# A new hand-searched order for a fused attention and gated-MLP kernel, with the normalization of v taken off GpSimd and two scalar loads issued late

## The chip, the cores and the metric

One Trainium2 chip; the program runs on one of its cores. The metric is device time in microseconds (us), the median of several runs. A profiled execution gives the trace from which the rows below are taken.

## The reference, cut to what matters

```python
# attention: B=4, H=8, S=768, D=64; the first 4 keys (sinks) and a window of 128 keys are kept
scores = scale * q @ k.T
keep = (pos < n_sink) | ((rel >= 0) & (rel < window))
a = exp(where(keep, scores, -1e9) - max); a = a / (sum(a) + 1e-9)
x = (a @ v).transpose(0, 2, 1, 3).reshape(B, S, 512)
# gated MLP: d_ff = 1024
h = maximum(x @ w_in, 0); u, v = h[..., :512], h[..., 512:]
v_n = (v - mean(v)) / sqrt(var(v) + 1e-6)          # over the last axis
v_s = einsum('ts,bsd->btd', w_spatial, v_n) + b_spatial[None, :, None]
out = (u * v_s) @ w_out
```

n_sink and window arrive as 64-bit integers, w_in and w_out as 64-bit floats.

## The kernel before, in words

The four batches b are cut into six blocks t of 128 rows. For each block and each half of the heads (hf) there is one piece of work of each kind: a score product on TensorE into four PSUM banks (tile `sc`), four masks on VectorE that also give the row maximum (`pexp`, `nm`), four exponentials on ScalarE, a split of the result into two 16-bit parts (`p`), a transpose, and the product with v (`av`). Then follow the block's `x`, its half of the first MLP product that gives v (`ps_v`), the relu into `vr`, the statistics on VectorE, the "root" (the power -1/2 of the variance, one GpSimd instruction, `rs`), the "norm" (subtract the mean, multiply by the root) and the split into `vn`. `ps_u`, `ps_s`, `ps_o` are the other products of the MLP; `ps_s` of a batch needs all six `vn` of it. Three PSUM banks serve the MLP products, so TensorE can be three such products ahead of the engines that read them.

At the start the weights are decoded: each 128x512 piece of w_in is loaded as 512 KB of 64-bit words (`dec`), and three engines make 32-bit floats of it: `wtmp` on ScalarE (L546), `w` on VectorE (L548, L551), the sum on GpSimd (L554). The first two blocks work on 32-bit data, the later ones on 16-bit pairs. The first key and query block is loaded in four pieces of 128 KB, two each on the queues of SyncE (SP) and ScalarE; all other loads and all transposes go through SP's queue.

No scheduler decides the order. `plan.add` gathers some 1,800 numbered pieces of work, each with the engines that may do it, and the table `ORDER` lists them in the order in which they are recorded: a number, a letter for the engine (d VectorE, a ScalarE, p GpSimd, P TensorE, S the SP queue), and for some TensorE pieces a count of filler matmuls (`P22`: 22 small products with the identity, line L438, ahead of the piece). Each engine takes its own pieces strictly in this order. The durations given to `plan.add` play no part when the kernel is built.

`load_scalars` brings the two scalar words n_sink and window to all partitions (`words`). They are read by one late VectorE piece (`wf`, L650) that goes into the flag which tells whether the fast path's result holds.

Of the kernel before, what the change touches and what calls it, by code (L numbers as in the profile page):

```python
# [6 lines left out]
F32 = mybir.dt.float32  # L7
# [3 lines left out]
I32 = mybir.dt.int32  # L11
# [8 lines left out]
P = 128  # L20
# [218 lines left out]
185P22:188 171P 214a 8a 221a 37d 225d 30d 157d 36a 108a 223a 234a 29a 31d 224p 256S 226S 222S 32p 10d 11p 187d
232a 230a 236a 237a 57S 50a 239a 238S 210a 261P 268d 262d 266d 188P3 189a 264d 241d 240p 242S 51d 109d 38d 39p  # L240
211d 144P 145d 12a 33a 269a 265a 263a 267a 270p 277P2:192 280d 284d 282d 363S 278d 34d 192P 272a 273p 52d 53p
227P 274d 318P 323d 271S 190a 191d 244d 283a 243P 281a 259a 275S 285a 40a 279a 286a 54p 193a 324a 325d 326a 290p
288a 289p 321d 322a 319d 320a 329a 497S 330p 245d 260d 55d 327a 331p 41d 313S 316a 146P 334P 341d 342a 337d 335d
246P 5a 339d 340a 194d 276P 201P 202a 336a 147a 247a 13d 317d 287S 367P 374d 6d 372d 368d 370d 293d 195p 196p
291S 338a 19a 343a 20d 345a 346p 205P 206a 203P 347p 248d 148d 292P 294d 383P 388d 362S 390d 384d 249P 498a 369a
371a 505S 386d 56S 328S 332S 333P 506p 550S 344S 63a 64d 375a 507p 373a 376a 378a 379d 348S 295P 204a 377S 380d
149p 150p 381S 387a 151p 197p 552S 510P 515d 511d 152p 517d 296d 513d 199P 297d 385a 349P 389a 391a 392a 394a
553p 395p 350d 351d 250a 251d 393S 200a 396p 397S 524P 525d 514a 365a 58S 305P 366d 298P 529d 531d 527d 554p 306a
# [69 lines left out]
1764d 1765a 1766d 1754P 1755a 1313S 1756S 1287S 1767P 1768d 1769p 1770a 1772P 1773d 1774p 1656P 1654P 1655a 1771d  # L318
1775d 1776d 1783P 1784d 1785p 1793P 1794d 1786a 1787d 1652P 1653d 1788P 1789d 1790p 1791d 1780P 1781a 1782S 1792d
1795p 1777P 1796a 1797d 1657a 1798P 1799d 1778a 1800p 1808P 1803P 1801a 1802d 1810P 1813a 1779S 1814S 1804P 1805a  # L320
1806S 1807P 1809P 1811d 1812S
"""


# [919 lines left out]
```

## Time and profile before

| what | value |
|---|---|
| median of 3 runs | 399.76 us (399.09 to 400.67) |
| the profiled execution's own time | 400.12 us |
| its span, first to last instruction | 398.3 us |
| TensorE busy | 387.3 us, 97% of the span |
| mean granted TensorE clock | 0.994 |

The span is shorter than the execution's own time by 1.8 us, which lie outside the instructions. A busy TensorE also counts a matmul that has been started and whose end is modelled, and it counts the filler matmuls.

### The profile page before, as it was taken

How to read it: one execution, taken by the hardware profiler on the slowest of the kernel's cores; microseconds unless marked ns; L12 is line 12 of the kernel's file. 1: busy time of each engine (PE TensorE's matmuls, PEld its weight loads, DVE VectorE, ACT ScalarE, POOL GpSimd, SP SyncE). 2: the span in 40 equal slices, each digit the busy share in tenths (PEclk: the TensorE clock that was granted, in tenths of full speed). 3: DMA queues.
4: the chain of work that ended last, by engine and by line, in shares of the span. 5: the costliest groups of instructions: out<-in, count | busy, mean ns of one | idle time of the engine just before them, and what ended most of it. 6: DMA issues, size and time to landing. Idle time of an engine off the chain costs nothing.

```text
span 398.3 us, 10079 instructions
## 1 busy us (share of the span) xinstructions
PE 387.3 (97%) x3682; PEld 276.9 (70%) x3682; DVE 323.4 (81%) x927; ACT 257.2 (65%) x726; POOL 220.2 (55%) x242
## 2 busy tenths in 40 slices
PE   7999999899999999999999999999999999999995
PEld 4686676567786866577786767567785776586863
DVE  1899999799999999989899978889888899642231
ACT  2899897589679985887988658577852143111111
POOL 4347999597653775736693847483553543400210
PEclk9899999999999999999999999999999999999999
DMA  5999899999997979899999698698978985001102
GB/s 167 358 289 212 170 240 180 231 248 228 232 286 137 230 160 235 159 233 184 173 224 155 115 167 148 132 229 173 150 198 225 249 220 127 12 18 53 54 28 84
DMA packets 137767, 70.84 MB, mean 178 GB/s; under 512 B 112112, under 2 KB 125424, under 8 KB 137712
## 3 DMA queue, kind: packets, MB, share of 16 engines
q1 hardware_dynamic: 136880, 69.88, 79.4%
q8 instruction: 30, 0.49, 0.5%
q10 hardware_dynamic: 832, 0.26, 0.3%
q14 instruction: 25, 0.20, 0.2%
HBM read 36.57 MB, written 6.29 MB: 108 GB/s over the span
## 4 chain that ended last, share of the span: by engine, by line
PE 75%; DMA 9%; DVE 7%; ACT 5%; POOL 2%; issue 1%; SPq 1%; ACTq 0%; POOLq 0%; DVEq 0%
PE ps_s L527 23%; PE ps_o L1101 15%; PE ps_v L527 11%; PE ps_u L527 11%; PE sc L772 7%; DMA pT<-p 3%; ACT pexp L783 2%; DMA dec<-w_in 2%; PE av L898 2%; PE av L899 2%; PE av L900 2%; DVE pexp L777 2%; DMA kring<-qk_t 2%; DMA wsp<-w_sp_t 2%; DMA pexp<-w_in 1%
## 5 line engine op out<-in xcount | busy, mean ns | idle before, releaser
L783 ACT ACTIVATE pexp<-pexp,nm 128x260 f32<-128x260 f32 (+1 forms) x192 | 92.6, 484 | 18.6 <-DVE nm L777 18.4
L527 PE MATMUL ps_s<-wsp,vn 128*128 128x256 f16 x864 | 100.0, 273 | 0.0
L527 PEld LDWEIGHTS <-vn 128*128 128x128 f16 x864 | 83.5, 98 | 13.5 <-issue 1.5
L527 PE MATMUL ps_u<-xT,win 128*128 128x256 f16 x576 | 69.4, 273 | 0.3 <-ACT u L1051 0.2
L509 POOL TENSOR_TENSOR p<-pexp,p 128x16 f16<-128x16 f32 (+2 forms) x40 | 49.4, 1244 | 31.3 <-ACT p L493 24.4
L527 PEld LDWEIGHTS <-win 128*128 128x128 f16 x576 | 54.6, 98 | 12.1 <-issue 3.8
L1101 PE MATMUL ps_o<-wout,g 128*128 128x512 f16 x276 | 62.7, 379 | 0.0
L527 PE MATMUL ps_v<-win,xT 128*128 128x512 f16 x264 | 60.5, 379 | 0.0
L772 PE MATMUL sc<-kring 64*128 64x260 f16 (+3 forms) x480 | 46.9, 319 | 2.4 <-DVE nm L777 1.7
L1078 POOL TENSOR_TENSOR g<-g,u 128x256 f32<-128x256 f32 x27 | 22.1, 819 | 47.8 <-DVE g L1074 47.0
L1101 PEld LDWEIGHTS <-g 128*128 128x128 f16 x276 | 26.5, 98 | 29.6 <-issue 1.0
L527 PEld LDWEIGHTS <-xT 128*128 128x128 f16 x264 | 25.1, 98 | 28.4 <-issue 0.4
L1074 DVE SCALAR_TENSOR_TENSOR g<-ps_s,b_bc 128x256 f32<-128x256 f32 x48 | 20.0, 418 | 28.7 <-PE ps_s L527 28.6
L493 ACT CAST p<-pexp 128x32 f16<-128x32 f32 (+2 forms) x63 | 36.2, 595 | 5.3 <-DMA pT<-p 4.4
L783 ACT ACTIVATION_READ_ACCUMULATOR pexp<-pexp,nm 128x1 f32 x192 | 36.3, 189 | 0.0
L1017 POOL TENSOR_SCALAR vr<-vr,mv,rs 128x512 f32<-128x512 f32 x15 | 33.9, 2257 | 1.2
L675 ACT ACTIVATE g<-g 128x256 f16<-128x256 f32 x21 | 8.7, 413 | 39.8 <-POOL g L1078 22.6
L898 PE MATMUL av<-vring,pT 128*128 128x64 f16 x328 | 32.9, 193 | 0.0
L900 PE MATMUL av<-vring,pT 128*128 128x64 f16 x328 | 32.7, 193 | 0.0
L899 PE MATMUL av<-vring,pT 128*128 128x64 f16 x328 | 32.7, 193 | 0.0
L509 DVE TENSOR_TENSOR p<-pexp,p 128x1024 f16<-128x1024 f32 (+2 forms) x36 | 31.9, 898 | 0.5 <-ACT p L493 0.3
L898 PEld LDWEIGHTS <-pT 128*128 128x128 f16 x328 | 29.4, 98 | 1.9 <-issue 1.1
(146 smaller groups left out, 735.4 us busy)
## 6 DMA issues: line engine op xcount, KB each, us to landing
vraw<-v_s SPq DMA_DIRECT2D x30, 256.0 KB, 3.9
raw<-qk_t SPq DMA_DIRECT2D x12, 512.0 KB, 4.4
out<-ob SPq DMA_DIRECT2D x23, 256.0 KB, 2.4
kring<-qk_t SPq DMA_DIRECT2D x11, 512.0 KB, 6.9
dec<-w_in SPq DMA_DIRECT2D x8, 512.0 KB, 8.0
pexp<-w_in SPq DMA_DIRECT2D x8, 512.0 KB, 4.4
wsp<-w_sp_t SPq DMA_DIRECT2D x6, 384.0 KB, 4.1
dec<-w_out SPq DMA_DIRECT2D x4, 512.0 KB, 4.3
```

Source lines behind the costliest of these rows:

```text
L493: nc.scalar.copy(o, x)
L509: eng[e].tensor_tensor(out=o, in0=x, in1=hi, op=ALU.subtract)
L527: nc.tensor.matmul(o, a, m, start=(i == 0), stop=(i == n - 1))
L772: nc.tensor.matmul(view(h + q)[0], qq[:, hp, 1, 2:], keys, start=(j == 0), stop=(j == len(pairs) - 1))
L783: nc.scalar.activation(po, po, AF.Exp, bias=nm()[:, q:q + 1], scale=-1.0, accum_out=small_tile("sums", (b, t), H)[:, k:k + 1])
L898: nc.tensor.matmul(o[:, h], ph, vh, start=(t < 2 and j == 0), stop=False)
L899: nc.tensor.matmul(o[:, h], ph, vl, start=False, stop=False)
L900: nc.tensor.matmul(o[:, h], pl, vh, start=False, stop=(j == nb - 1 and (t < 2 or h == HH - 1)))
L1017: eng[e].tensor_scalar(vr(), vr(), vals["mv", i][:, 0:1], vals["rs", i], op0=ALU.subtract, op1=ALU.mult)
L1074: nc.vector.scalar_tensor_tensor(out=g(), in0=tl("ps_s", i)[:, :TC], scalar=G_S, in1=b_bc[:, t0:t0 + TC], op0=ALU.mult, op1=ALU.add)
L1078: eng[e].tensor_tensor(out=g(), in0=g(), in1=tl("u", (b, c0))[:, d, :], op=ALU.mult)
L1101: nc.tensor.matmul(o, lead, wout[:, w, d, :], start=(d == 0 and j == 0), stop=(d == KC - 1 and j == 2))
```

## The change

Four things change. The two word loads go from ScalarE's queue at the very start to SP's queue late in the program. The norm of v may run on ScalarE (as `scale * x + bias`) or VectorE instead of VectorE or GpSimd; for this, the root piece makes one more GpSimd value, `nb` = minus mean times root. The costs that the search for the order was given change at a few places. And the whole `ORDER` table is another one; its first two lines stand here for all 88.

```diff
 def load_scalars(nc, words, n_sink, window):
-    nc.scalar.dma_start(words[:, 0:2], n_sink.bitcast(I32).partition_broadcast(P))
-    nc.scalar.dma_start(words[:, 2:4], window.bitcast(I32).partition_broadcast(P))
+    nc.sync.dma_start(words[:, 0:2], n_sink.bitcast(I32).partition_broadcast(P))
+    nc.sync.dma_start(words[:, 2:4], window.bitcast(I32).partition_broadcast(P))
...
-114S 118P16 119d 123d 125d 124a 21S 23d 126a 121d 122a 120a 115S 116p 258p 209p 130P10:129 137d 22a 154S 110S
+114S 110S 118P12 115S 116p 117p 155p 111a 112d 121d 123d 119d 120a 125d 130P6:129 133d 135d 124a 122a 126a 127P
...
-            plan.add("check", last, 0, "d", 0.4, words, [], [("good", 0, 2)])
+            plan.add("w check", last, 0, "SP", 0.9, st.load_words, [], [("words", 0)], dma=2.0)
+            plan.add("check", last, 0, "d", 0.4, words, [("words", 0)], [("good", 0, 2)])
...
             def root(e):
-                nc.gpsimd.tensor_tensor(out=vals["rs", i], in0=vals["rs", i], in1=mhalf, op=ALU.pow)
+                rs = vals["rs", i]
+                nc.gpsimd.tensor_tensor(out=rs, in0=rs, in1=mhalf, op=ALU.pow)
+                vals["nb", i] = small.tile([P, 1], F32, tag="nb", name="nb")
+                nc.gpsimd.tensor_scalar(vals["nb", i], vals["mv", i][:, 0:1], rs, -1.0, op0=ALU.mult, op1=ALU.mult)
 
             def norm(e):
-                eng[e].tensor_scalar(vr(), vr(), vals["mv", i][:, 0:1], vals["rs", i], op0=ALU.subtract, op1=ALU.mult)
+                if e == "a":
+                    nc.scalar.activation(vr(), vr(), AF.Identity, bias=vals["nb", i], scale=vals["rs", i])
+                else:
+                    nc.vector.tensor_scalar(vr(), vr(), vals["mv", i][:, 0:1], vals["rs", i], op0=ALU.subtract, op1=ALU.mult)
...
-            plan.add("v root", r, b, "p", 0.535, root, [], [("st", i)])
-            plan.add("v norm", r, b, "dp", {"d": 0.47, "p": 2.05}, norm, [("st", i)], [("vr", i)], shared=True)
+            plan.add("v root", r, b, "p", 1.05, root, [], [("st", i)])
+            plan.add("v norm", r, b, "ad", {"a": 0.72, "d": 0.47}, norm, [("st", i)], [("vr", i)], shared=True)
...
-            load_scalars(nc, words, n_sink, window)
...
+            st.load_words = lambda e: load_scalars(nc, words, n_sink, window)
```

Counted over the two tables: of the 24 norms 15 stood on GpSimd and 9 on VectorE, and now 20 stand on ScalarE and 4 on VectorE; the filler matmuls go from 69 to 54 (16 to 12 ahead of the first scores, 10 to 6 ahead of the second, 12 to 8 and 22 to 14 around the first `av` products). Some 200 other pieces change their engine, in both directions; on balance VectorE gets 5 more low parts of `p` (28 of 44 instead of 23) and 6 more relus of u, and gives up 6 small sink parts.

VectorE at the start of the program, before: the masks of the first block (`m_first`, each with its `nm` row), and between them the first step of decoding weights.

```order
L777 ISA pexp,nm<-sc,m_first 128x128
L777 ISA nm 128x1
L548 TENSOR_SCALAR w_175<-dec 128x512
L777 ISA pexp,nm<-sc,m_first 128x128
L777 ISA nm 128x1
```

VectorE at the same place, now: the last mask of the first block, then the decoding, then the first mask of the second block (`m_second`).

```order
L778 ISA pexp,nm<-sc,m_first 128x128
L778 ISA nm 128x1
L548 TENSOR_SCALAR w_208<-dec 128x512
L551 SCALAR_TENSOR_TENSOR w_208<-dec,w_208 128x512
L778 ISA pexp,nm<-sc,m_second 128x260
```

Before, the decoding step stood ahead of five of the first block's eight masks; now it stands behind all eight. Ahead of the first mask there is now one step that waits for the small load `vsraw` (not in these rows).

ScalarE at the start, before: its two loads of the first keys, the two word loads, the table load, then the exponentials of the first block (L783) and the first decoding steps (L546).

```order
L1192 DMA kring<-qk_t 128x2x128 x2
L35 DMA words<-n_sink 128x2
L36 DMA words<-window 128x2
L1196 ACT_TABLE_LOAD
L1196 ACTIVATE first<-first 128x1
L783 ACTIVATE pexp,sums<-pexp,nm 128x128 x4
L546 ACTIVATE wtmp<-dec 128x512
L783 ACTIVATE pexp,sums<-pexp,nm 128x128 x4
L694 ACTIVATE vsink_134<-vsraw 96x256
```

ScalarE at the start, now, up to the first exponentials of the second block:

```order
L1199 DMA kring<-qk_t 128x2x128 x2
L1202 ACT_TABLE_LOAD
L1202 ACTIVATE first<-first 128x1
L695 ACTIVATE vsink_132<-vsraw 96x256
L784 ACTIVATE pexp,sums<-pexp,nm 128x128 x4
L546 ACTIVATE wtmp<-dec 128x512
L818 COPY pT<-pt 128x512
L784 ACTIVATE pexp,sums<-pexp,nm 128x128 x4
L546 ACTIVATE wtmp<-dec 128x512
L784 ACTIVATE pexp,sums<-pexp,nm 128x260 x2
```

The two word loads are gone from here, the step on `vsraw` came to the front, and the copy of the first transposed block (`pT`) came over from VectorE.

VectorE near the end, now, where the words are read (`wf`): the gates of the last batch (L1081) around it each free a bank of `ps_s`.

```order
L1081 SCALAR_TENSOR_TENSOR g<-ps_s,b_bc 128x256
L1093 SCALAR_TENSOR_TENSOR g_5931<-g_5931,g 128x256
L638 TENSOR_SCALAR good<-checks 128x31
L639 TENSOR_SCALAR good<-checks 128x12
L640 TENSOR_SCALAR good<-checks 128x12
L641 TENSOR_SCALAR good<-checks 128x12
L650 CAST wf<-words 128x4
L652 TENSOR_SCALAR good<-wf 128x1 x4
L1081 SCALAR_TENSOR_TENSOR g<-ps_s,b_bc 128x256
```

The reading of the words waited for nothing recent before; now it stands ahead of a gate and waits for a load that the SP queue issues some pieces earlier: in the table, TensorE has a `ps_u` and a `ps_s` between that issue and this row.

## Rows read from the trace of the kernel before

**Rows 1.** The page's first part: busy us, share of the span, instructions.

```profile
PE 387.3 (97%) x3682; PEld 276.9 (70%) x3682; DVE 323.4 (81%) x927; ACT 257.2 (65%) x726; POOL 220.2 (55%) x242
```

**Rows 2.** Waits of TensorE: us in total, times, longest.

```profile
PE pt L946 <- ACT vr L1001: 1.7, 1, 1.7
PE sc L772 <- DVE nm L777: 1.7, 1, 1.7
PE sc L772 <- DMA kring<-qk_t: 0.8, 1, 0.8
```

**Rows 3.** Windows: busy us of each engine, granted clock, DMA share, GB/s.

```profile
5.00:10.00 5.00, 3.81 (x25) 2.69 (x24) 1.03 (x7) 0.88 (x4) 0.80 (x6) 1.00 0.65 202
10.00:15.00 5.00, 4.10 (x19) 2.82 (x20) 3.22 (x16) 3.96 (x15) 1.88 (x2) 0.66 1.07 360
20.00:40.00 20.00, 19.95 (x183) 14.95 (x180) 19.81 (x58) 19.51 (x56) 12.01 (x13) 1.00 0.96 250
60.00:80.00 20.00, 17.56 (x183) 12.48 (x183) 16.70 (x57) 13.73 (x42) 15.28 (x16) 1.00 1.18 203
100.00:200.00 100.00, 100.00 (x1023) 70.36 (x1022) 93.70 (x251) 83.58 (x236) 63.11 (x64) 1.00 0.98 204
340.00:398.00 58.00, 53.97 (x405) 39.42 (x403) 19.59 (x49) 9.28 (x20) 10.35 (x15) 0.99 0.12 43
```

**Rows 4.** DMA issues of the first 4 us: queue, size, us to landing.

```profile
kring<-qk_t SPq DMA_DIRECT2D x1, 512.0 KB, 9.6
words<-n_sink ACTq DMA_DIRECT2D x1, 1.0 KB, 8.1
```

**Rows 5.** Timeline of the first 17 us, SP, ScalarE and VectorE: start, duration, what.

```profile
1.80 0.49 ACTq L35 DMA_DIRECT2D words<-n_sink  x1
2.25 0.67 SPq L736 DMA_DIRECT2D kring<-qk_t  x1
...
6.08 0.29 DVE L777 CUSTOM_DVE_ANT_0 pexp<-sc,m_first 128x128 f32<-128x128 f32 x1 [5.12 <-PE sc L772]
...
9.78 0.43 DVE L548 TENSOR_SCALAR w<-dec 128x512 int32<-128x512 int32 x1 [2.88 <-DMA dec<-w_in]
...
16.00 0.51 ACT L783 ACTIVATE pexp<-pexp,nm 128x260 f32<-128x260 f32 x1
```

**Rows 6.** Timeline of TensorE, first 31 us.

```profile
6.29 1.89 PE L438 MATMUL av<-ident 128*128 128x248 f16 x10
...
10.47 0.48 PE L772 MATMUL sc<-kring 64*128 64x128 f32 x2 [1.66 <-DVE nm L777]
...
13.05 1.84 PE L772 MATMUL sc<-kring 64*128 64x260 f32 x8
...
23.90 2.50 PE L438 MATMUL pt<-ident 128*128 128x248 f16 x22
```

**Rows 7.** Groups by line and form: count, busy us, mean ns.

```profile
L783 ACT ACTIVATE pexp<-pexp,nm 128x128 f32<-128x128 f32 x32 | 12.5, 392 | 7.9 <-DVE nm L777 7.8
L546 ACT ACTIVATE wtmp<-dec 128x512 int32<-128x512 uint32 x12 | 8.0, 667 | 0.9 <-DMA dec<-w_in 0.4 <-POOL w L554 0.4
L495 ACT ACTIVATE win<-w 128x512 f16<-128x512 f32 x6 | 3.6, 618 | 0.0
L817 ACT COPY pT<-pt 128x512 f32<-128x512 f32 x4 | 2.1, 577 | 0.7 <-PE pt L813 0.7
L1017 POOL TENSOR_SCALAR vr<-vr,mv,rs 128x512 f32<-128x512 f32 x15 | 33.9, 2257 | 1.2
L1014 POOL TENSOR_TENSOR rs<-rs,mhalf 128x1 f32<-128x1 f32 x24 | 18.4, 767 | 18.5 <-DVE rs L1011 17.5 <-DVE sums L905 1.0
L509 POOL TENSOR_TENSOR p<-pexp,p 128x1024 f16<-128x1024 f32 x17 | 36.8, 2163 | 22.1 <-ACT p L493 15.5 <-issue 5.9 <-DVE p L498 0.6
```

**Rows 8.** The chain that ended last, a late stretch: start, us, what.

```profile
378.34 1.31 PE ps_u L527 x12
379.65 1.97 PE ps_s L527 x18
```

More of the change, by code (lines that the diff above doesn't have):

```diff
@@ L239 @@
[L239 to L248, printed above, removed]
@@ L319 @@
[L319 to L321 removed]
+114S 110S 118P12 115S 116p 117p 155p 111a 112d 121d 123d 119d 120a 125d 130P6:129 133d 135d 124a 122a 126a 127P
+131d 137d 21S 22a 23d 24d 154S 158P3:129 25p 159d 163d 161d 165d 42S 44d 128a 132a 138a 134a 136a 142d 113S 129P
+45d 28S 30d 139P 43a 172P1:169 173d 177d 175d 179d 162a 160a 31d 140a 141P 143d 164a 166a 169P 167P 168d 207S
@@ new lines @@
+210a 208S 209p 46p 212P 215d 219d 174a 29a 176a 153S 156p 180a 217d 213d 32p 47p 48d 178a 181P8 183P 7S 8a 9d
+186d 35S 37d 10d 211d 228P 231d 235d 229d 233d 216a 220a 14S 258p 0S 2d 157d 11p 16d 107S 184a 170a 214a 218a
+223a 224p 3d 171P2 315p 256S 17d 221a 225d 15a 18p 182a 1a 4p 185P14:188 187d 257S 261P 262d 266d 268d 264d 362S
+234a 108a 259a 232a 236a 230a 237a 36a 260d 244d 49S 50a 188P6 189a 314S 222S 144P 239a 277P2:192 226S 238S 241d
+240p 242S 51d 284d 192P 52d 363S 109d 227P 33a 267a 265a 53p 263a 269a 272a 273p 270a 271S 280d 278d 279a 282d
@@ new lines @@
+283a 34d 274d 275S 54a 145a 193a 281a 38d 55d 318P 319d 321d 323d 39p 285a 243P 245d 286a 288a 325d 290d 313S
+146P 190p 191d 287S 320a 324a 289p 291S 326a 322a 334P 5a 147a 327a 40p 41d 329a 246P 247a 26p 364p 337d 335d
+341d 342a 339d 19p 331p 148d 149p 276P 336a 199P 200a 338a 340a 343p 347p 330d 293d 367P 372d 374d 368d 369a 370d
+371a 316a 345a 346p 365a 27d 194d 56S 550S 248d 292P 294d 205P 20d 328S 332S 373a 375a 317d 383P 206a 12a 13d 6d
+386d 366d 388d 201P 202a 378a 379p 376a 203P 295P 390d 296a 297d 150a 151a 195p 384d 344S 505S 506p 387a 607p
@@ new lines @@
+1352d 841a 1485S 856P 1433a 1355a 1351a 863p 1217S 1348d 1349a 1332d 999p 864a 1000a 1107d 1353a 1001a 1342p
+1344p 1213S 1430S 1108d 1109S 857d 858p 859p 1202P 1382P 1385d 1386a 1487a 1007P 1389d 1390a 1383d 1008a 860d
+1387d 1388a 1384a 1057P 865d 1218P 1220d 1356p 1358p 1396P 1397d 1403d 1343S 1401d 1404a 842S 1345S 1399d 763a
+1400a 1373S 1435d 1391d 1393d 877P 878d 1486a 1168a 1169d 1398a 1402a 869P 870a 1439P 1440d 1444d 1346P 1058d
+1359S 1597S 1357S 1446d 1442d 1599S 1317S 1405a 1406S 1407d 1123P 1124a 1443a 1447a 1005P 872P 1360P 1059d 871S
@@ new lines @@
+1744p 1745p 1746d 1747P 1748d 1652P 1653d 1749p 1750a 1751d 1758P 1759d 1760d 1316S 1761a 1762d 1755P 1756a 1763P
+1764d 1768P 1765d 1766p 1767d 1726d 1769d 1729d 1752P 1753a 1754S 1757S 1770d 1771a 1772d 1730P 1731d 1773P 1774d
+1775d 1776a 1777d 1784P 1785d 1786d 1654P 1655d 1787p 1788d 1781P 1794P 1795d 1796p 1789P 1790d 1791p 1792a 1793d
+1782a 1783S 1313S 1778P 1779a 1780S 1656P 1657d 1797d 1798d 1799P 1809P 1800d 1801p 1802d 1803d 1804P 1811P 1814a
+1815S 1805P 1806a 1808P 1810P 1812d 1807S 1813S
```

141 lines of the change are left out of this document (66 added, 75 removed).

## The prediction

> **What bounds the kernel now.** The page's busy times come first [rows 1]: TensorE is busy 97% of the span, so whatever is won must be won where TensorE waits, or where it runs fillers. The list of its waits [rows 2] names 4.2 us at three places. The windows [rows 3] place them: from 100 to 200 us TensorE is busy 100.00 of 100, from 60 to 80 only 17.56 of 20, and from 5 to 15 only 7.91 of 10, with fillers inside (10 of them take 1.89 us from 6.29 [rows 6]). So there are three stretches with air: the opening (to about 30 us), 60 to 80, and the end. Between them the reader should see that nobody else has air at once: from 20 to 40 TensorE, VectorE and ScalarE are busy 19.95, 19.81 and 19.51 of 20 [rows 3]. A lead that these three have at 20 us is therefore a lead that no engine has idle time to lose again, and it goes through to the end.
>
> In the opening, the timeline [rows 5, 6] tells one story. The first mask runs at 6.08. Then VectorE stands 2.88 us at the first decoding step until 9.78, when the first weight piece has landed; five masks stand behind it in the queue. Behind those masks TensorE waits 1.66 us for a bank, ScalarE for its exponentials: ScalarE is busy 0.88 us from 5 to 10 and 3.96 from 10 to 15 [rows 3], and the second block's first exponential starts at 16.00. Behind all of it stands the memory: from 5 to 10 us the loads run at 202 GB/s, from 10 to 15 at 360 [rows 3]. What is different in the slow stretch is that the two word loads are in flight: 1 KB each, issued at 1.80 and just after, landed 8.1 us later [rows 4, 5], that is at 9.9.
>
> **The change part by part.**
>
> *The head of the queues.* I price the lead at one mark, the second block's first exponential, at 16.00 before.
>
> Upper end: the loads run at 360 GB/s from 5 us on. What moved in 5 us at 202 then takes 2.8, so everything that landed near 10 lands 2.2 us sooner: the first weights near 7.6, plus 0.3 for the 96 KB of `vsraw` that now go ahead of them; the second block's keys, issued at 2.25 and 9.6 us on the way [rows 4, 5], at about 10.0 instead of 11.9. The masks no longer wait for the weights. They wait for `vsraw`, a small load right behind the first keys, and two short steps on it; I put the first mask at 6.1 to 6.5 instead of 6.08 and the first exponential at 6.7. ScalarE then has 8 short exponentials (0.392), two decoding steps (0.667) and the copy taken over from VectorE (0.577) ahead of the mark [rows 7]: 5.05 us, so 6.7 + 5.05 = 11.75, and with some 0.3 of waits 12.1. The keys at 10.0 allow that. The lead is 3.9.
>
> Lower end: the words did not slow anything. The first weights land at 9.78 + 0.3; ScalarE's decoding step, copy, four exponentials take to 12.9; the next decoding step needs the second weight piece, which follows the keys (11.9 + 0.3) by 512 KB at 360 GB/s, 1.5 us, so 13.7; with the step itself the mark is at 14.3. The lead is 1.7, and this is what the new order wins by itself.
>
> I take **3.2**: nearer to the upper end, since the slow rate begins and ends with the words [rows 3, 5], with a discount because ScalarE's queue is strict and each of five pieces there must arrive in time.
>
> One rule of the Trainium skill speaks against this part. DMA: Bandwidth & Descriptors, section Queues, rings and completion order, says that each DMA engine takes turns between the queues, packet by packet; two 1 KB loads on another queue would then cost the large loads a few short turns. By that rule the lead would be near 1.7, and the time near 396.5.
>
> *Fillers.* Behind the mark, 7 fewer stand in the queue, mostly 14 for 22 around the first `av` products. 22 take 2.50 us [rows 6], 0.11 each, so 0.8 us. They cost only where TensorE has nothing better; half, **0.4** (0 to 0.8). The 4 fewer before the first scores are worth nothing, since the masks behind wait for `vsraw`.
>
> *The norm.* 15 GpSimd norms of 2.257 us go (33.9 us [rows 7]). The second value of the root is not in the trace; by the nearest rows on GpSimd it costs at most the 0.767 of the root itself, at least nothing: 0 to 18 us over 24. ScalarE gets 20 norms; the nearest row is a plain 128x512 split at 0.618 [rows 7], so 12 us or some more; in 100 to 200 it is busy 83.58 of 100 and hides them. GpSimd, busy 15.28 of 20 from 60 to 80, is relieved exactly where TensorE waits: there TensorE stands 1.7 us for a transposed block behind ScalarE and 0.8 for keys [rows 2], with the DMA share at 1.18 [rows 3], so part of it is the memory and stays. Of the 2.44 us that TensorE is not busy from 60 to 80 I take half, **1.2** (0 to 2.4).
>
> *The late words.* Reading them now waits for a load. If it takes 8.1 us again, with the DMA share at 0.12 in that stretch [rows 3], the cover is this: TensorE has a `ps_u` (1.31) and a `ps_s` (1.97) [rows 8] between the issue and the waiting row on VectorE, and then a `ps_s` and a `ps_u` more until its three banks are full, 6.6 us. A load in an idle stretch should be well under 8.1, and SP has little in front of it: 0, at worst 1.5 lost.
>
> Moving the other 200 pieces between engines I price at nothing; their work is the same and TensorE's is identical; VectorE's sum of gains and losses is about 1 us in 323.
>
> Sum: 3.2 + 0.4 + 1.2 = **4.8** off the profiled execution's 400.12, so 395.3. The median of the runs is 0.36 under that execution, so the median comes to **395.0**.
>
> **Rivals.**
>
> *The loads come no sooner.* By the packet rule above. For it: the words are 2 KB. Against it: the 202 against 360 GB/s, with the words in flight in one and not in the other. Lead 1.7 instead of 3.2: 396.5.
>
> *The lead is lost again.* The memory is busy from 20 on too (0.96, later 1.18 [rows 3]), and transposes share its queue; a new order can put a large load ahead of an urgent transpose at any place. For it: exactly such a wait cost the 1.7 and 0.8 us of 60 to 80. If the opening gives only 1.7 and a like pair of waits arises somewhere else, 400.12 - 1.7 = 398.4, as a median 398.0, within what can be told from no change.
>
> *Slower: ScalarE waits for GpSimd.* A norm on ScalarE stands in a strict queue, and the root before it is on GpSimd behind whatever is there, often a low part of `p` of 2.163 us [rows 7]. While ScalarE waits, the exponentials behind it wait, then masks' banks, then TensorE. In 100 to 200 ScalarE has 16.4 us idle [rows 3]; six norms of one batch fall there and take 3.7. So it decides above (16.4 - 3.7) / 6 = 2.1 us of wait each. A root behind a low part costs 2.16 + 0.77 + 0.5 = 3.4: 20.6 us against 12.7 that are free, 7.9 lost in that batch, 403. Against it: a good order puts the root early, and in the table the statistics stand well ahead of the norm.
>
> *The words stop the end.* 8.1 of landing against 6.6 of cover: 1.5 lost, 396.5.
>
> **How the numbers follow.** Forecast as summed: 45%. Loads no sooner: 21%. Lead lost: 17%. ScalarE behind GpSimd: 11%. Words at the end: 6%. The likeliest gives the time, 395.0. The ends of its unknowns are 3.9 + 0.8 + 2.4 = 7.1 off, 392.7, and 1.7 off, 398.0. The range takes in both and what lies a little past them, for the case that the lead is all lost or that other stalls close: 391.8 to 399.2; what it leaves out is the slow rival and a little at the low end, under 2 in 10. A measurement of this kernel can tell about 0.5%, 2 us, from no change. Faster by more: nearly all of the first case, most of the second, nearly all of the last and a small part of the third, 0.71. Within 0.5%: most of the third and the rest, 0.19. Slower: the ScalarE rival in the main, 0.10.
>
> **What would show it.** In the changed profile: the first weights landing near 8 and not 10, with over 300 GB/s from 5 to 10 us; no wait of VectorE for them ahead of masks; the second block's first exponential near 12.8; TensorE at 100% from about 27 us; under 2 us of TensorE waits from 55 to 80; no norm on GpSimd; little idle time of ScalarE put down to the root; VectorE waiting at the reading of the words without a wait of TensorE behind it. Wrong it would be if the first weights landed at 10, if TensorE showed idle time after 80 us, or if the mark moved and the end did not: then the bound between 20 and 90 us is not the three engines but the memory.

## The result and the profile after

The changed kernel takes **397.64 us** (median of 20 runs: 19 from 394.34 to 399.96, and one of 1006.45 that no other repeats); the kernel before, on the same chip, 401.35 (397.82 to 405.31). The ratio is **0.9908, 95% interval 0.9887 to 0.9929**: 3.7 us less, with an interval of 2.8 to 4.5. Ratios, here and below, leave out the few runs that took over 1.5% longer than the fastest of their kernel. The forecast was 395.0 with a range of 391.8 to 399.2. From profiled execution to profiled execution the gain is 4.27 us (400.12 to 395.85; span 394.1).

Windows of the kernel after; the columns are those of [rows 3].

```profile
5.00:10.00 5.00, 3.65 (x26) 2.62 (x25) 3.33 (x19) 2.72 (x11) 0.33 (x3) 0.88 1.01 314
10.00:15.00 5.00, 5.00 (x32) 3.37 (x30) 2.95 (x14) 4.25 (x16) 1.45 (x3) 0.78 1.09 362
20.00:40.00 20.00, 19.55 (x161) 13.73 (x162) 19.87 (x59) 19.87 (x56) 11.08 (x11) 1.00 1.04 218
60.00:80.00 20.00, 18.96 (x199) 13.59 (x197) 17.55 (x57) 18.65 (x56) 12.59 (x16) 1.00 1.14 230
80.00:100.00 20.00, 19.43 (x196) 15.16 (x192) 17.94 (x50) 16.46 (x45) 14.11 (x17) 1.00 1.00 223
100.00:200.00 100.00, 100.00 (x1068) 70.88 (x1066) 92.99 (x258) 86.15 (x235) 56.08 (x75) 1.00 0.91 194
300.00:340.00 40.00, 39.66 (x337) 27.81 (x335) 32.33 (x90) 14.19 (x32) 11.89 (x17) 1.00 0.84 199
```

For two of these stretches the windows of the kernel before were not shown yet:

```profile
80.00:100.00 20.00, 19.90 (x203) 14.59 (x204) 19.33 (x50) 18.08 (x50) 16.94 (x16) 1.00 1.00 238
300.00:340.00 40.00, 39.91 (x318) 27.43 (x315) 36.21 (x107) 11.04 (x27) 15.85 (x17) 1.00 0.77 197
```

From 5 to 10 us the loads run at 314 GB/s instead of 202 [rows 3]. From 60 to 80 TensorE gains 1.40 us; from 80 to 100 it gives 0.47 of that back, from 300 to 340 another 0.25. And its granted clock, 1.00 and 0.66 in the two stretches of the opening before [rows 3], is 0.88 and 0.78. In windows of 1 us it is 1.00 (2.4 GHz) or 0.50 (1.2 GHz) but for those in which it changes, so a mean of 0.88 says that a part of the window ran at half. Nothing in the prediction speaks of it.

TensorE's waits in the kernel after (in total, times, longest), where [rows 2] had three of 1.7, 1.7 and 0.8:

```profile
PE av L893 <- DMA pT<-p: 1.0, 1, 1.0
PE sc L773 <- DVE nm L778: 1.0, 1, 1.0
PE ps_u L527 <- ACT u L1058: 0.6, 1, 0.6
```

The opening of the kernel after, from the timelines of ScalarE, VectorE and TensorE (as [rows 5, 6]; lines stand one or more further down):

```profile
6.00 0.42 ACT L695 ACTIVATE vsink<-vsraw 96x256 f16<-96x256 f32 x1 [2.71 <-DMA vsraw<-v_sink]
13.34 0.51 ACT L784 ACTIVATE pexp<-pexp,nm 128x260 f32<-128x260 f32 x1 [0.75 <-DVE nm L778]
...
6.45 0.42 DVE L697 SCALAR_TENSOR_TENSOR vsink<-vsraw,vsink 32x256 f16<-32x256 f32 x1 [5.48 <-ACT vsink L695]
6.90 0.29 DVE L778 CUSTOM_DVE_ANT_0 pexp<-sc,m_first 128x128 f32<-128x128 f32 x1
8.85 0.42 DVE L548 TENSOR_SCALAR w<-dec 128x512 int32<-128x512 int32 x1
...
7.25 1.12 PE L773 MATMUL sc<-kring 64*128 64x128 f32 x8 [1.01 <-DVE nm L778]
10.47 1.96 PE L773 MATMUL sc<-kring 64*128 64x260 f32 x8
```

The masks no longer wait for the weights, but the two steps on `vsraw` hold the first of them to 6.90. The second block's score starts at 10.47 (13.05 before [rows 6]), yet it takes 1.96 us. At full clock a score of this form takes 1.15, as the runs below show. The windows of 1 us say why:

```profile
9.00:10.00 1.00, 1.00 (x5) 0.79 (x6) 0.97 (x2) 0.96 (x4) 0.00 (x0) 0.50 1.02 392
10.00:11.00 1.00, 1.00 (x5) 0.56 (x5) 0.00 (x1) 1.00 (x4) 0.85 (x1) 0.50 1.06 414
11.00:12.00 1.00, 1.00 (x8) 0.74 (x4) 0.18 (x1) 1.00 (x7) 0.55 (x2) 0.50 1.02 383
```

TensorE stood still for 1.01 us before 7.25, and from 9 to 12 it runs at half. The mark, the second block's first exponential, comes at 13.34.

The late words cost nothing. The two loads are issued by SP at 339.17 and 339.65, land 3.5 and 3.8 us after issue (the first of them after 8.1 in the opening before [rows 4]), and VectorE reads them without a wait:

```profile
351.33 0.16 DVE L650 CAST wf<-words 128x4 f32<-128x4 int32 x1
```

### The profile page after: what moved, and what is told of

Same layout as the page of the kernel before. It is cut to its first block, busy times and chain, and to the rows that moved or that the text cites. A ratio compares the mean times of both kernels' runs of the same rounds, so it can differ in the third digit from the quotient of the medians.

```text
span 394.1 us, 10057 instructions
## 1 busy us (share of the span) xinstructions
PE 383.9 (97%) x3667; PEld 274.6 (70%) x3667; DVE 317.7 (81%) x921; ACT 269.3 (68%) x739; POOL 191.1 (48%) x259
## 5 line engine op out<-in xcount | busy, mean ns | idle before, releaser
L509 POOL TENSOR_TENSOR p<-pexp,p 128x16 f16<-128x16 f32 (+2 forms) x41 | 43.9, 1076 | 25.5 <-ACT p L493 24.8
L1085 POOL TENSOR_TENSOR g<-g,u 128x256 f32<-128x256 f32 x24 | 18.9, 789 | 54.1 <-DVE g L1081 54.0
L493 ACT CAST p<-pexp 128x1024 f16<-128x1024 f32 (+1 forms) x64 | 38.4, 621 | 3.6 <-DMA pT<-p 3.0
L509 DVE TENSOR_TENSOR p<-pexp,p 128x1024 f16<-128x1024 f32 (+2 forms) x35 | 36.2, 1038 | 2.2 <-ACT p L493 1.2
L1081 DVE SCALAR_TENSOR_TENSOR g<-ps_s,b_bc 128x256 f32<-128x256 f32 x48 | 20.1, 419 | 18.4 <-PE ps_s L527 17.6
L899 PE MATMUL av<-vring,pT 128*128 128x64 f16 x328 | 33.2, 193 | 0.0
L1093 DVE SCALAR_TENSOR_TENSOR g<-g,g 128x256 f16<-128x256 f16 x48 | 24.5, 516 | 10.8 <-ACT g L676 6.7
L901 PE MATMUL av<-vring,pT 128*128 128x64 f16 x328 | 33.2, 193 | 0.0
L900 PE MATMUL av<-vring,pT 128*128 128x64 f16 x328 | 33.1, 193 | 0.0
L554 POOL TENSOR_TENSOR w<-w,wtmp 128x512 int32<-128x512 int32 x12 | 17.0, 1422 | 28.3 <-DVE w L551 23.2
```

Source lines behind the costliest of these rows:

```text
L493: nc.scalar.copy(o, x)
L509: eng[e].tensor_tensor(out=o, in0=x, in1=hi, op=ALU.subtract)
L899: nc.tensor.matmul(o[:, h], ph, vh, start=(t < 2 and j == 0), stop=False)
L900: nc.tensor.matmul(o[:, h], ph, vl, start=False, stop=False)
L901: nc.tensor.matmul(o[:, h], pl, vh, start=False, stop=(j == nb - 1 and (t < 2 or h == HH - 1)))
L1081: nc.vector.scalar_tensor_tensor(out=g(), in0=tl("ps_s", i)[:, :TC], scalar=G_S, in1=b_bc[:, t0:t0 + TC], op0=ALU.mult, op1=ALU.add)
```

## The experiments

Each ratio is to the kernel before on the same chip. "Clock" is the mean granted clock over all runs of a row (the kernel before: 0.993 to 0.995 on the chips used); the third score and the mark are start times in the profiled execution.

| kernel | ratio, interval | clock | 5 to 10 us, GB/s | third score | mark |
|---|---|---|---|---|---|
| before | 1 | 0.993 | 202 | 13.05 | 16.00 |
| after | 0.9908, 0.9887 to 0.9929 | 0.9945 | 314 | 10.47 | 13.34 |
| e1: before, words late | 0.9949, 0.9925 to 0.9974 | 0.998 | 290 | 11.15 | 13.96 |
| e2: after, words early | 1.0003, 0.9967 to 1.0039 | 0.987 | 205 | 11.73 | 14.71 |
| e3: after, thin loads | 0.9906, 0.9861 to 0.9950 | 0.994 | 255 | 10.48 | 12.54 |
| e4: after, words twice early | 1.0109, 1.0055 to 1.0163 | 0.985 | 133 | 13.39 | 16.38 |
| e5: before, norms of after | 1.0323, 1.0278 to 1.0368 | 0.987 | 197 | 11.01 | 13.99 |
| e6: after, norms of before | 1.0291, 1.0242 to 1.0340 | 0.984 | 320 | 11.18 | 14.21 |
| e7: after, vsraw steps later | 0.9940, 0.9902 to 0.9978 | 0.991 | 307 | 10.25 | 12.00 |
| e10: after, 17 more fillers | 0.9957, 0.9930 to 0.9984 | 0.995 | 302 | 10.80 | 12.88 |
| e11: e7 and 21 more fillers | **0.9853, 0.9813 to 0.9893** | 0.998 | 309 | 10.03 | 11.79 |
| e12: after, two loads moved | 0.9926, 0.9898 to 0.9954 | 0.9905 | 303 | 10.85 | 13.60 |
| e14: e11, words early | 0.9935, 0.9900 to 0.9970 | 0.9955 | 219 | 12.08 | 13.84 |
| e15: e11, 30 fillers fewer | 0.9921, 0.9890 to 0.9953 | 0.992 | 293 | 10.00 | 11.76 |

### Do the two word loads slow the opening?

**e1**, the change's late words alone (the order of before stays, with the load as a piece of SP's near the end):

```diff
-            load_scalars(nc, words, n_sink, window)
...
+            plan.add("w check", last, 0, "SP", 0.9, st.load_words, [], [("words", 0)], dma=2.0)
```

> The kernel before, in its own order, with one part of the change alone: the two word loads leave the opening and are issued by SP near the end. Theory A (the words slow the large loads while they are in flight): from 5 to 10 us the loads run at more than 300 GB/s instead of 202, the first weights land near 8.2 instead of 9.76, the second block's first exponential comes at 14.0 to 14.8 instead of 16.00, and the time is 1.0 to 2.0 us less (ratio 0.995 to 0.9975). Theory B (two loads of 1 KB cost the others a few short turns, and the opening was won by the new order of the queues): 202 GB/s, weights at 9.8, mark at 16.0, ratio 1.000.

Measured: 0.9949, theory A in the time and nearly in the rate (290); the mark (13.96) fits too, but see e5. The mean clock is 0.998 against 0.993, which over 400 us is up to 2 us of work. So this run's 2.0 us (1.0 to 3.0) can't be split between loads that come sooner and a clock that falls less.

```profile
5.00:10.00 5.00, 3.26 (x27) 2.36 (x26) 1.50 (x10) 1.57 (x7) 0.79 (x6) 1.00 0.94 290
10.00:15.00 5.00, 4.76 (x38) 3.60 (x38) 4.75 (x23) 4.69 (x19) 1.90 (x2) 1.00 1.08 360
```

**e2**, the reverse: the changed kernel with the words early, on ScalarE's queue again.

```diff
                 (nc.sync, nc.scalar)[h % 2].dma_start(kring[:, 0, h:h + 1, :, 2:], qk[0, 0, :, h:h + 1])
+            load_scalars(nc, words, n_sink, window)
...
-            st.load_words = lambda e: load_scalars(nc, words, n_sink, window)
+            st.load_words = lambda e: None
```

> The changed kernel with the same part undone: the two word loads go out on ScalarE's queue behind the first keys, as in the kernel before; the late load does nothing. Theory A: from 5 to 10 us about 200 to 220 GB/s instead of 314, first weights near 10.2 instead of 8.54, second block's keys near 12 instead of 10.34, the mark at 14.5 to 15.3 instead of 13.34, ratio to the kernel before 0.993 to 0.997. Theory B: as the changed kernel, 314 GB/s, mark at 13.3, ratio 0.991.

Measured: 1.0003. The rate (205) and the mark (14.71) are those of theory A; the time is worse than it allowed. The whole gain is gone. (The profiled execution, 398.91, is the fastest of its 12 runs, so its mark, 1.3 us earlier than before, can't be set beside the median.) Against the profiled execution of the changed kernel, whose order it has, e2 is 1.4 us behind at the mark and 3.0 at the end. The windows of e2 show what lies between:

```profile
5.00:10.00 5.00, 3.40 (x27) 2.24 (x23) 2.51 (x18) 2.27 (x10) 0.32 (x2) 1.00 0.73 205
10.00:15.00 5.00, 3.32 (x15) 2.54 (x15) 2.53 (x11) 3.44 (x12) 1.40 (x2) 0.68 1.06 373
15.00:20.00 5.00, 5.00 (x29) 3.81 (x29) 3.10 (x14) 4.18 (x14) 1.94 (x2) 0.64 1.07 388
```

TensorE waits 1.68 us for the second block's keys, the clock falls, and from 10 to 20 us it gives 3.4 us less than full speed, twice the 1.7 that the changed kernel loses from 5 to 15 (0.88 and 0.78) and the kernel before from 10 to 15 (0.66 [rows 3]).

**e3** and **e4** add loads to the changed kernel, in the same place on ScalarE's queue: e3 the two words into one partition, e4 both words into 128 partitions, twice.

```diff
+            nc.scalar.dma_start(spare[:, 0:2], n_sink.bitcast(I32).partition_broadcast(1))
+            nc.scalar.dma_start(spare[:, 2:4], window.bitcast(I32).partition_broadcast(1))
```

```diff
+            for j in range(2):
+                nc.scalar.dma_start(spare[:, 4 * j:4 * j + 2], n_sink.bitcast(I32).partition_broadcast(P))
+                nc.scalar.dma_start(spare[:, 4 * j + 2:4 * j + 4], window.bitcast(I32).partition_broadcast(P))
```

> The changed kernel plus two loads of the same words at the old place on ScalarE's queue, but into one partition each (8 bytes in all for each, not 8 bytes for each of 128 partitions), into a buffer that nobody reads. Theory A in its narrow form (what costs is the 128 pieces of 8 bytes): nothing changes, 5 to 10 us at 300 GB/s or more, weights at 8.5, mark at 13.3, ratio 0.991. Theory A2 (what costs is any small load on a second queue at that time): near 200 GB/s, weights at 10, mark near 15, ratio 0.994 to 0.997. Theory B: nothing changes either.

> The changed kernel plus the suspected cost twice: both word loads, spread over all 128 partitions, issued two times each at the old place on ScalarE's queue, into a buffer that nobody reads. Theory A: the slow stretch lasts longer than with one pair: about 200 GB/s from 5 to 10 us and still under 300 from 10 to 15 (362 in the changed kernel), first weights at 11 or later, mark at 16 or later, ratio 0.997 to 1.003. Theory B: a few more short turns, rate above 290, mark at 13.4, ratio 0.991.

Measured: e3 0.9906, as the changed kernel (its rate of 255 was lower than expected, the third score and the mark were not later); e4 1.0109, worse than expected. Windows of e4:

```profile
5.00:10.00 5.00, 3.08 (x22) 2.09 (x21) 2.54 (x18) 3.43 (x11) 0.39 (x4) 0.91 0.46 133
10.00:15.00 5.00, 2.93 (x14) 1.91 (x13) 1.05 (x3) 3.25 (x13) 1.40 (x2) 0.50 1.03 379
15.00:20.00 5.00, 5.00 (x25) 3.74 (x21) 3.18 (x14) 3.06 (x11) 1.59 (x2) 0.50 1.09 372
20.00:40.00 20.00, 19.80 (x136) 15.54 (x133) 17.38 (x55) 16.64 (x47) 8.49 (x10) 0.85 0.73 201
```

So it is not just any small load on a second queue that costs, but one that is spread as 8 bytes to each of 128 partitions. e3 differs from the words at once in partitions, pieces and bytes; which of these counts, and whether the words early on SP's own queue would cost the same, was not tried. And the engines are not busy with it: their share from 5 to 10 us is 0.65 to 0.74 in the four executions with one pair, 0.46 with two, 0.94 to 1.01 in the nine others. The queues from 5 to 10 us (packets, MB, share of 16 engines; q10 is ScalarE's): the first two lines are of the kernel before, the third is of the changed kernel, the last two are of e4.

```profile
q1 hardware_dynamic: 1004, 1.01, 62.1%
q10 hardware_dynamic: 286, 0.00, 2.8%
...
q1 hardware_dynamic: 1376, 1.57, 100.8%
...
q1 hardware_dynamic: 609, 0.66, 42.2%
q10 hardware_dynamic: 362, 0.00, 3.4%
```

The small packets themselves take 2.8 and 3.4%. An estimate from these lines: 0.35 and 0.54 of 16 engines' 5 us stay idle, which is 0.10 and 0.12 us for each of the 286 and 362 small packets, of 8 ns each.

Theory B (turns between queues) falls with e1, e2 and e4. Two expectations missed: e4's rate from 10 to 15 was 379, not under 300, so the slow stretch grew deeper, not longer; and its time was worse, by the half clock up to 20 us and beyond.

### The norms

**e5** is the kernel before with the norms' engines and the root of the change; **e6** the changed kernel with those of before. Each norm keeps its place in the order. The edits, with one of the 20 changed letters of the order:

```diff
-            plan.add("v norm", r, b, "dp", {"d": 0.47, "p": 2.05}, norm, [("st", i)], [("vr", i)], shared=True)
+            plan.add("v norm", r, b, "ad", {"a": 0.72, "d": 0.47}, norm, [("st", i)], [("vr", i)], shared=True)
...
-196p
+196a
```

> The kernel before, words early and in its own order, with the norm part alone: the 24 norms run on ScalarE or VectorE as in the changed kernel, each at the place in the program where it stood, and the root makes the second value. Theory C (GpSimd relieved from 60 to 80 us is worth about 1.2 us): TensorE busy 18.7 instead of 17.56 from 60 to 80, ratio 0.9965 to 0.9985. Theory D (the norm part by itself is worth nothing here, what TensorE waits for is the memory): 60 to 80 stays at 17.6, ratio 1.000. Rival for the worse (ScalarE waits for the root): TensorE under 99.5 of 100 from 100 to 200, ratio above 1.005.

> The changed kernel with the norm part undone: each norm back on the engine that it had before (15 of them on GpSimd), no second value at the root; order and late words stay. Theory C: GpSimd's low parts come late, TensorE near 17.6 to 18 from 60 to 80 us instead of 18.96, ratio to the kernel before 0.993 to 0.996 instead of 0.991. Theory D: ratio 0.990 to 0.992. Since this order was made for norms elsewhere, a GpSimd norm of 2.26 us may also stand in the way of a low part at a later place: then waits of TensorE at p or vn after 100 us and a ratio above 0.996.

Measured: 1.0323 and 1.0291. From 60 to 80 us e5 is as theory D said (17.39); its time and its 96.61 from 100 to 200 are those of the rival for the worse. e6 is as theory C said from 60 to 80, with the ratio of its last case. First two windows of e5, then two of e6:

```profile
60.00:80.00 20.00, 17.39 (x176) 12.17 (x176) 16.14 (x51) 15.24 (x47) 13.25 (x16) 1.00 1.05 218
80.00:100.00 20.00, 16.59 (x139) 11.70 (x136) 13.61 (x37) 14.89 (x39) 9.21 (x10) 0.91 0.86 204
```

```profile
60.00:80.00 20.00, 17.59 (x196) 12.74 (x194) 14.79 (x48) 14.22 (x42) 13.27 (x13) 1.00 1.15 211
100.00:200.00 100.00, 97.05 (x986) 67.62 (x983) 92.21 (x246) 77.77 (x218) 62.84 (x68) 1.00 0.93 187
```

With GpSimd's norms gone and the old order kept, 60 to 80 stays at 17.39 (17.56 in [rows 3]), and TensorE loses 3.3 us from 80 to 100 and 3.4 from 100 to 200. With the norms put back into the new order, 60 to 80 falls to 17.59 and 100 to 200 to 97.05. So what is gained there comes of the norms and the order together; neither has it alone. Its size scatters: in the ten profiled executions with both, TensorE is busy 17.8 to 19.0 of 20 (mean 18.5), in the four others 17.1 to 17.6.

The loss of e5 has a cause that its chain shows in part. At 81 us the chain of work that ended last goes through GpSimd's root (`nb` is its second value) and a norm on ScalarE to the exponentials behind it:

```profile
81.27 0.28 POOL nb L1017
81.57 0.81 ACT vr L1021
82.39 0.50 ACT pexp L783 x2
```

And in the other direction GpSimd's steps on `vn` wait 22.5 us for ScalarE's norms, at 6 places (6.3 at 4 in the changed kernel). How much of e5's 13 us this makes up, and what e6 loses after 100 us, was not followed further.

e5 showed something else. Its opening is that of the kernel before, instruction by instruction up to the mark, words early, 197 GB/s. Yet in its profiled execution the words land 5.6 and 6.4 us after issue, the weights are there at 7.24, not 9.78, and the mark is at 13.99, not 16.00 [rows 4, 5]:

```profile
words<-n_sink ACTq DMA_DIRECT2D x1, 1.0 KB, 5.6
...
7.24 0.43 DVE L548 TENSOR_SCALAR w<-dec 128x512 int32<-128x512 int32 x1 [0.74 <-DMA dec<-w_in]
13.99 0.51 ACT L783 ACTIVATE pexp<-pexp,nm 128x260 f32<-128x260 f32 x1
```

So the landing of one load, and with it the mark, moves by 2 us between executions of the same opening, and e5's mark with the words early is e1's with the words late. What holds in every execution is the rate from 5 to 10 us: 197 to 219 GB/s in the four with one pair of words early, 255 to 320 in the nine without. A mark of one execution can't carry the case for e1 or e2; their timed runs and this rate do.

### The opening's first steps, and the clock

**e7**: the steps on `vsraw` go behind the first exponential (ScalarE) and the sixth mask (VectorE), and ScalarE's exponentials stand in the order of their masks.

```diff
-117p 155p 111a 112d 121d 123d 119d 120a 125d 130P6:129 133d 135d 124a
+117p 155p 121d 123d 119d 120a 111a 125d 130P6:129 133d 135d 112d 124a
...
-162a 160a
+160a 164a
...
-164a 166a
+162a 166a
```

> The changed kernel with the two steps on vsraw moved behind the first exponential on ScalarE and behind the sixth mask on VectorE, and ScalarE's four exponentials of the second block put in the order of their masks. Theory E (the first masks wait for vsraw, and with them TensorE's second score): first mask at 5.3 to 5.8 instead of 6.90, no wait of 1.0 us of TensorE for a bank at 6 to 7 us, granted clock above 0.9 from 8 to 12 us instead of 0.50 to 0.88, the second block's first exponential at 11.8 to 12.7 instead of 13.34, ratio to the kernel before 0.986 to 0.9885. Theory F (the mark hangs on the keys that land at 10.3 and the memory behind them): first mask earlier, mark at 12.6 or later, time as the changed kernel, ratio 0.990 to 0.992.

Measured: first mask at 5.24, mark at 12.00, as theory E said, and the ratio 0.9940, no better than the changed kernel. Its 12 runs, time and mean granted clock:

```
394.75 1.000   395.08 1.000   395.35 1.000
398.00 0.991   398.40 0.991   399.63 0.990   399.98 0.987   400.07 0.991
400.20 0.986   400.36 0.986   400.43 0.985   400.63 0.987
```

The same program takes 395 us where the clock holds and 398 to 400.6 where it falls. A mean of 0.986 over 398 us is 5.6 us of work lost, and the two groups stand 3 to 5.5 apart. The clock is not the whole of a run's time, though: runs of the changed kernel at 0.999 to 1.000 took from 394.34 to 399.36. The profiled execution is of the second group. TensorE's timeline:

```profile
10.25 1.15 PE L773 MATMUL sc<-kring 64*128 64x260 f32 x8 [1.60 <-DMA kring<-qk_t]
12.21 1.94 PE L887 MATMUL av<-vraw,pT 128*128 128x64 f32 x8 [0.81 <-ACT wtmp L546]
```

It works sooner, so it waits longer for the keys, 1.60 us; behind 0.81 more its clock is at half (0.50 from 15 to 20 us).

**e10** leaves the changed kernel's steps where they are and adds fillers.

```diff
-130P6:129
+130P18:129
...
-158P3:129
+158P8:129
```

> The changed kernel with 17 more fillers in TensorE's two waits of the opening: 18 instead of 6 ahead of the second score, 8 instead of 3 ahead of the third. Theory G (part of the lead is lost because TensorE's granted clock falls to half after its waits at 6 and 8 us, and the third score then runs at half speed): granted clock 0.95 or more from 5 to 15 us instead of 0.88 and 0.78, third score in 1.1 to 1.2 us instead of 1.96, mark near 12.6, ratio to the kernel before 0.987 to 0.989. Theory H (the work behind waits for the loads anyway): clock up, but no gain, ratio 0.990 to 0.992; the third score may be pushed back by up to 0.5 us, ratio 0.992.

Measured: 0.9957, more than either theory allowed (H: up to 0.992). The clock is 1.00 from 5 to 15 us and the third score takes 1.15 us, as theory G said, but the 18 fillers take 3.33 us and push the second score from 7.25 to 8.72, the third from 10.47 to 10.80. The fillers outlast the wait: the first mask comes at 5.91. That this eats what the clock gives is likely, but not shown: the profiled execution, the fastest of 12, still reaches the mark 0.46 us sooner than the changed kernel, and what makes the timed runs some 2 us slower was not found.

**e11**: e7, with fillers cut to its waits.

```diff
-127P
+127P5
...
-158P3:129
+158P14:129
...
-129P
+129P5
```

> The kernel with the steps on vsraw moved back (the run e7_after_vsink_later), plus 21 fillers in TensorE's three waits of its opening: 5 ahead of the first transposes, 14 instead of 3 ahead of the third score, 5 ahead of the first av product. Theory G (what separates the runs of one kernel, and what took the gain of the moved steps, is TensorE's granted clock falling to half after waits in the opening: in 12 runs of e7 those at a mean clock of 1.000 took 394.8 to 395.4 us, those at 0.985 to 0.991 took 398.0 to 400.6): mean granted clock 0.996 or more in nearly all runs, 1.00 from 10 to 20 us, time 394.5 to 396, ratio to the kernel before 0.984 to 0.988. Theory H (the clock only follows from waits that the loads set, and fillers win nothing): clock up, time as e7, ratio 0.992 to 0.996.

Measured: **395.75 us, 0.9853**, theory G. All 6 runs are at 0.996 or more. Its interval ends at 0.9893, and 0.9887 is where that of the changed kernel begins: most likely a little better than the changed kernel, clearly better than the kernel before. Its windows, and its timeline at the third score:

```profile
10.00:15.00 5.00, 4.78 (x37) 3.61 (x38) 3.71 (x16) 3.87 (x14) 2.08 (x3) 1.00 1.09 363
15.00:20.00 5.00, 5.00 (x45) 4.16 (x46) 5.00 (x20) 4.79 (x17) 2.59 (x5) 1.00 1.03 392
```

```profile
8.20 1.65 PE L438 MATMUL av<-ident 128*128 128x248 f16 x14
10.03 1.15 PE L773 MATMUL sc<-kring 64*128 64x260 f32 x8 [0.18 <-DMA kring<-qk_t]
```

**e14** is e11 with the words early again (the edit of e2); **e15** is e11 without the fillers of 16 to 28 us:

```diff
-181P8
+181P
...
-171P2
+171P
...
-185P14:188
+185P
...
-188P6
+188P
```

> The run e11_vsink_later_fills (steps on vsraw moved back, 21 fillers more in the opening, 0.9853 to the kernel before) with the two word loads put back on ScalarE's queue behind the first keys. If the early words cost by the late landing of keys and weights alone, with the clock held by the fillers: 200 to 210 GB/s from 5 to 10 us, third score at 11.5 to 12 instead of 10.03, mean clock 0.995 or more, time 397.0 to 397.9, ratio 0.989 to 0.992. If they cost by the late landing and by the clock that falls in the longer wait: third score as said, granted clock near 0.5 to 0.7 somewhere from 10 to 20 us, mean clock 0.985 to 0.990, time 399 to 402, ratio 0.994 to 1.001.

> The run e11_vsink_later_fills without the 30 fillers at 16 to 28 us (8, 2, 14 and 6 at four places; those of the opening stay). As the prediction priced fillers (0.11 us each, half of them in the way): 1.6 us less, ratio 0.981. If they only fill waits for ScalarE (behind the 14 TensorE still waits 0.2 us for a transposed block): TensorE waits there by their time, no gain, ratio 0.985. If they hold the granted clock: under 0.9 from 20 to 30 us, the loss half of what runs at half speed, 1 us or more, ratio 0.988 or above.

Measured: e14 0.9935, 3.3 us worse than e11 by the ratios, between the two cases: TensorE waits 2.04 us for the keys behind the 14 fillers, the clock is 0.75 and 0.91 from 10 to 20 us, but the mean over the runs falls by only 0.3 to 1 us of work (0.9955 to 0.9972 for 0.998). So of the words' price (1.2 to 5.4 us by the intervals) the larger part is here the late keys, a smaller part the clock. e15 0.9921, the third case, the opposite of my price for fillers:

```profile
20.00:25.00 5.00, 2.10 (x16) 1.82 (x16) 4.75 (x17) 4.97 (x15) 1.89 (x3) 1.00 1.09 332
25.00:30.00 5.00, 4.92 (x24) 4.37 (x24) 3.08 (x5) 4.97 (x15) 3.35 (x2) 0.55 1.30 187
30.00:35.00 5.00, 5.00 (x25) 3.22 (x22) 4.60 (x17) 3.99 (x15) 0.22 (x1) 0.77 0.53 107
```

Without them TensorE is busy 2.10 of 5, then its clock falls to 0.55 and 0.77, 3.4 us of work in the profiled execution; by the ratios the loss is 2.7 (0.7 to 4.7).

### The wait at 62 us

**e12**: a load of `w_sp` and one of `v` go behind the transposing transfers.

```diff
-57S 503S 552S
+552S
...
-381S
+381S 57S 503S
```

> The changed kernel with one move in the middle: a load of w_sp and a load of v, which SP issues at 53.2 and 53.9 us ahead of a load of keys and four transposing transfers of p, go behind the second of those. Theory J (the part of the lead lost at 62 us, where TensorE waits 1.0 us for a transposed block, is the transfer standing behind loads that nobody needs yet): that wait falls under 0.3 us, TensorE above 19.5 of 20 from 60 to 80 us instead of 18.96, ratio 0.987 to 0.990. Theory K (the memory is the limit there, 1.14 of DMA share, and a wait closed there opens at the next transposed block or at w_sp): another wait of 0.5 us or more before 100 us, ratio 0.990 to 0.993.

Measured: 0.9926, and TensorE still waits 1.2 us for the transposed block (1.0 to 2.2 in the profiled executions of this order); theory J falls, and no other wait takes its place as theory K had it: the wait stays. The transfer's own data come late. GpSimd's step on `p` waits for ScalarE's cast:

```profile
58.05 0.62 POOL L509 TENSOR_TENSOR p<-pexp,p 128x16 f16<-128x16 f32 x1 [1.79 <-ACT p L493]
```

SP issues the second transfer at 58.66, as this ends, and it lands 4.4 us later. With VectorE busy 19.21 and ScalarE 18.26 of 20 from 40 to 60 in the changed kernel, there is little room to make `p` sooner.

## Why the prediction came out as it did

The number held: 397.64 lies in the range, and faster was the likeliest case. Of the 2.6 us that it lies above the forecast, 1.6 come of the base: the kernel before, 399.76 in the three runs that the forecast started from, took 401.35 here. The gain was smaller than the sum, 3.7 us (2.8 to 4.5) for 4.8, and the terms are not all what they were taken for.

**The words slow the loads: right.** 314 GB/s for "over 300", VectorE's first decoding step at 8.85 with no wait ahead of it, no mask of the first block behind the weights. The rival "the loads come no sooner" is refuted by e1, e2 and e4. With four such loads the engines' share falls from 1.01 to 0.46, and e3 shows that the spread form of the load is what matters. The Trainium skill's DMA: Bandwidth & Descriptors, section Queues, rings and completion order, has the engines take turns between queues; by that alone they would have stayed busy, and the traces differ. The same page of the Trainium skill, section Specifications, names 512 B as the least transfer at full rate. The words' pieces are of 8 bytes, and the traces agree in direction; no run shows the mechanism that the page gives.

**The opening lead: 3.2 predicted, 2.66 at the mark of the two profiled executions.** Two steps failed. One is "I price the lead at one mark", at 16.00: e5 has 13.99 with the same opening, so the terms of 3.9, 3.2 and 1.7 were measured from one late execution. The safer size is that of timed runs, with what the clock adds to it: late words 2.0 us in the old order (e1), 3.8 (2.1 to 5.5) in the new (e2 against the changed kernel). The other is "The keys at 10.0 allow that". It ended the chain of the mark at ScalarE's queue. But behind the keys stand a score, three masks (ScalarE's first exponential of that block belongs to the third mask) and only then the mark, 2.87 us from 10.47 to 13.34. The score ran at half clock, 1.96 us instead of 1.15. The first mask came at 6.90 instead of 6.1 to 6.5, because the two steps on `vsraw` follow each other on two engines; e7 shows 5.24 without them ahead, and a mark at 12.00.

**"A lead that these three have at 20 us ... goes through to the end": right; but the lead at the mark is not yet the lead at 20 us.** Start times of ScalarE's exponentials by their place in its order (the 9th is the mark, the 192nd the last), and the end of the span:

| kernel | 9th | 17th | 192nd | end |
|---|---|---|---|---|
| before | 16.00 | 21.64 | 288.95 | 398.3 |
| e1 | 13.96 | 19.59 | 287.33 | 397.9 |
| after | 13.34 | 19.46 | 283.51 | 394.1 |
| e2 | 14.71 | 22.12 | 287.10 | 397.1 |
| e7 | 12.00 | 22.68 | 287.90 | 398.6 |

e1, in the order of before, keeps 1.6 of its 2.0 us to the last exponential and to the issue of the last store (only behind that issue is it lost: the span ends 5.0 us later, 3.8 before). In the changed kernel's order e2 and e7 have most of their loss by the 17th. Between the mark and the 17th lies the half clock: e7 is 1.3 us ahead of the changed kernel at the mark and 3.2 behind at the 17th. The prediction read the idle time of three engines and left out a fourth thing, TensorE's clock, which stood in [rows 3] (0.66 from 10 to 15); TensorE is busy at half speed just as at full. That this cost the sum nothing is luck: the changed kernel lost as much to it in its profiled execution as the kernel before, 1.7 us. The prediction took a mark that moves while the end does not for a sign of the memory; in e7 it is the clock.

The lower end of the lead, 1.7 "by itself", is refuted: with the words early, the rest of the change is worth nothing that can be told (1.0003, and its 17th exponential comes 0.5 us later than before). On top of late words it is worth 1.6 us (0.9949 to 0.9908; the intervals just touch).

**Fillers: 0.4 predicted; the price is wrong for those that stayed.** The step was "They cost only where TensorE has nothing better; half". It left out that they hold the clock up: e15 loses 2.7 us without 30 of them, at a mean clock of 0.992 for 0.998. What the 7 that the change takes out cost or gave, no run separates.

**The norms: 1.2 predicted, 1.40 from 60 to 80, 0.93 with what 80 to 100 gives back.** Size right as far as one execution tells (the mean of the ten is 1.0 more than before); the cause "GpSimd is relieved exactly where TensorE waits" is not enough, since e5 has the relief and not the gain. The rival of a ScalarE held up by the root did not happen in the changed kernel: its norms wait 5.7 us in 5 places, and TensorE is busy 100.00 from 100 to 200. In e5, where the order was not made for it, it did in part: the norms there wait 5.1 us, no more, but the work behind them on ScalarE and GpSimd waits in its turn, as the chain shows. TensorE's idle time after 80 us, which the prediction named as a sign of being wrong, is there too, but small: 0.57 of 20 us and 0.34 of 40.

**Late words at the end: 0, as predicted**; they land in 3.5 and 3.8 us, not 8.1. **"The lead is lost again"** came true in part: a wait of 1.0 us at 62 and one of 0.6 at 84 stand in place of two larger ones.

## What to carry to other kernels

Move a small load that is spread over all partitions out of a stretch in which the first large loads decide when work can start: two of 1 KB cost this kernel 2.0 to 3.8 us. In an opening read the granted clock in windows of 1 us beside the waits, and price a wait of the matrix engine at its length and at the half speed that may follow; fillers cut to the length of the waits kept the clock up here (e11, 0.9853), fillers that outlast a wait kept it up too but pushed the next work back (e10, 0.9957). Where a table fixes the order, an engine's load can't be moved alone: test the pair. And a landmark of one execution is worth as much as its scatter over several: read a lead behind the stretch in which the clock can fall, and take its size from timed runs.

## What the runs showed that was not expected

Two loads of 1 KB, 8 bytes to each of 128 partitions, leave the DMA engines idle and not busy: a share of 0.65 to 0.74 from 5 to 10 us with one pair, 0.46 with two, 0.94 to 1.01 with none, while large loads wait in another queue. By the estimate above, some 0.1 us of an engine's time goes with each small packet. Why, stays open. One program fell into two groups of time, told apart by its clock (e7: 395 at 1.000, 398.0 to 400.6 at 0.985 to 0.991); what decides in a run whether the clock falls after a given wait was not found. ScalarE's norm takes 0.809 us, not the 0.618 of the nearest row [rows 7], and the root's second value 0.509 on GpSimd in the mean (median 0.296).
